# Keys of batches 1 to 3: loaded once by rows, transposed in pairs of heads, copied by VectorE into padded and 56-query tiles

## The chip, the cores and the metric

The kernel runs on one core of one Trainium2 chip. Its time is the device time of one execution in microseconds (us). Several executions of a kernel are taken and their median is given. One further number comes from an execution under the hardware profiler, with a record of every instruction: the span in it runs from the first to the last instruction, and the execution's own time is a little longer than its span.

The engines are named as the profile names them: PE is TensorE (matmul), PEld its weight load, DVE is VectorE, ACT is ScalarE, POOL is GpSimd, and SP is SyncE, which only issues transfers here. [...]

## The reference

The computation is an attention followed by a mixture of four experts. Of eight heads, three ("retrieval": 0, 2, 6) see all earlier keys, and five ("streaming": 1, 3, 4, 5, 7) see the first 4 keys (the sinks) and the last 64.

```python
# q, k, v: (4 batches, 8 heads, 768 rows, 64); n_sink = 4, window = 64
scores = scale * np.matmul(q, k.transpose(0, 1, 3, 2))
causal = rel >= 0                       # rel = query row - key row
stream_keep = causal & (is_sink | (rel < window))
mask = np.where(is_retrieval, causal, stream_keep)
a = softmax(np.where(mask, scores, -1e9))
x = np.matmul(a, v)                     # heads side by side: (3072, 512)

p = domain_probs / (domain_probs.sum(-1, keepdims=True) + 1e-09)
for e in range(4):                      # 3072 tokens, 512 -> 1024 -> 512
    h = np.maximum(x @ w1[e], 0.0)
    out += p[:, e:e + 1] * (h @ w2[e])
```

## The kernel before

**Stages.** The attention is cut into eight stages g = 2b + c: batch b (0 to 3) and half c of its 768 rows (CH = 384 queries). A stage makes xT[g], 384 tokens by 512, which the experts use. The experts take tokens in pieces: 384 and 128 tokens the plain way (plain_steps; first layer L950, second L971), then ten pairs of 128 (pair_steps; first layer L1063, then a product of half-size blocks in seven parts, L1096, whose sums VectorE makes at L919, L1037 and L1117). The inputs of a pair are scaled by the probabilities, once for each expert: scale_inputs, L1029, into a double buffer xs.

**Order.** The order of each engine's instructions is written by hand, and each engine keeps it. attention(b, c) and moe_steps() are generators that yield an estimate of the TensorE time of what they have just issued. A loop at the end of the kernel advances the experts and puts in attention steps behind a plan (the table `plan`, with att_ns(a) as the assumed length of a stage). require(a) drains the stages up to a before their output is read. Work that should stand a little later in the order (the scaling of a streaming head's output, L762) goes through later() and is issued by tick() once 1300 ns of the estimate have gone by.

**A stage of batches 1 to 3** (by_dma, g = 2 to 7) takes its heads in the order 0, 2, 6, 1, 3, 5, 7, 4. scores(h), L627, multiplies key tiles with the transposed queries qT; ScalarE takes the exponential (L645) and VectorE multiplies by a mask (L649). values(h) or values_r(h), L739 and L675, follow one or two heads behind.

**Keys and queries.** Both have to lie with the head's 64 numbers on the partitions. Before the change:

- loads(g + 1) is called at the start of stage g. On POOL it loads the keys of the three retrieval heads (load_k, L229, into kRr, 128 x 3 x 64 each), the queries of all heads (L207, into q16, three transfers of 128 x 8 x 64), the retrieval heads' values, and the keys of the five streaming heads (L233, into kSr). These go in windows: seven tiles of 128 rows, each 55 rows beyond the last (WQ = 55), so that each key row is loaded about twice. The half of a key tile's columns that belongs to the other head of a pair is zero.
- After the fourth head of stage g (in stage 1: at its end), transpose_rows(g + 1) puts on SP three transposing transfers for the queries (L268) and one for kRr (L255, nine blocks of 128 x 128, into kR).
- After the last head's scores of stage g, transpose_windows(g + 1) puts on SP put_sinks for kSr (L249, in first halves only, and L250: the 4 sink rows into each of the seven windows) and one transposing transfer of kSr (L255, 35 blocks, into kS).

So each key tile of a stage was transposed by the DMA into the place from which PE reads it. kRr and kSr have one buffer each.

**Values** of streaming heads are loaded in windows too, one head after another as values(h) frees its tile (L281), and their sinks are put in by sink_rows after the second head of the stage (the same put_sinks). 

Of the kernel before, what the change touches and what calls it, by code (L numbers as in the profile page):

```python
# [17 lines left out]
def kernel(  # L18
# [34 lines left out]
    P = 128  # L53
# [22 lines left out]
    NT = S // TK  # L76
    TC = CH // TK
    assert NS <= R0 and NW == 64 and NS + NW <= TK
    WQ = 55
    WK = WQ + NW - 1  # L80
    WT = 7
    WO = P - WK + NW
    assert WT * WQ - 1 == CH and NS + WK <= P

    pers = ctx.enter_context(tc.tile_pool(name="pers", bufs=1))
    att = ctx.enter_context(tc.tile_pool(name="att", bufs=1))
# [55 lines left out]
    p_sb = pers.tile([P, NTILE, E], FP32, name="p_sb")  # L142


    kRr = pers.tile([P, NR, 3, P], FP16, name="kRr")
    kSr = pers.tile([P, WT, NSH, P], FP16, name="kSr")
    sinks = pers.tile([P, 1, NSH * P], FP16, name="sinks")
    k_sinks = sinks[0:NS, :, :]
    v_sinks = sinks[P // 2 : P // 2 + NS, :, :]

# [71 lines left out]
            ),  # L222
        )

    def load_k(b, c, heads):

        for h in heads:
            if RETR[h]:
                gp.dma_start(  # L229
                    out=kRr[:, RH.index(h), :, own(h)], in_=rows_of(k, b, h, c)  # L230
                )
            else:
                gp.dma_start(  # L233
                    out=kSr[:, :, SH.index(h), own(h)],
                    in_=windows_of(k, b, h, c),
                )

    qTs = {}

# [11 lines left out]
            out=x[0:NS, :, :], in_=src.to_broadcast([NS, WT, NSH * P])  # L251
        )

    def transpose_keys(x, xr):
        nc.sync.dma_start(  # L255
            out=x.rearrange("p t s x -> p (t s) x"),
            in_=xr.rearrange("p t s x -> p (t s x)"),
            transpose=True,
        )

    def transpose_windows(b, c):
        put_sinks(kSr, k_sinks, c)
        transpose_keys(windows(kSf), kSr)

    def transpose_rows(b, c):
        alloc_qT(b, c)
        for j in range(3):
            nc.sync.dma_start(  # L268
                out=qTs[b, c][:, :, j * P : (j + 1) * P],
                in_=q16[b, c][:, j, :, :].rearrange("p h d -> p (h d)"),  # L270
                transpose=True,
            )
        transpose_keys(kR[b % 2][:, c, :, :, :], kRr)

    def load_v(b, c, heads):
        for h in heads:
# [158 lines left out]
    def mask_w():  # L435


        gp.memset(mW, 1.0)
        gp.affine_select(
            out=mW, in_=mW, compare_op=ALU.is_ge, fill=0.0,  # L440
            base=NW - WO, pattern=[[0, WT + 2], [-1, WQ]], channel_multiplier=1,
        )
        gp.affine_select(
            out=mW, in_=mW, compare_op=ALU.is_ge, fill=0.0,
            base=WO - 1, pattern=[[0, WT + 2], [1, WQ]], channel_multiplier=-1,
        )
# [7 lines left out]
        gp.affine_select(  # L454
            out=mW[0:NS, 1, :], in_=mW[0:NS, 1, :], compare_op=ALU.is_ge, fill=0.0,
            base=WQ - 1 - NW, pattern=[[1, WQ]], channel_multiplier=-1,
        )

    mask_c(bC, 0.0, -60000.0)
# [48 lines left out]
    def attention(b, c):  # L508
# [72 lines left out]
        def score_tiles(h):  # L581
            if RETR[h]:
                if c == 0:
                    return [
                        (512, [(2, 0, 256, 128), (0, 128, 0, 384)], [(mC, 0, 0, 256)]),
                        (256, [(1, 0, 128, 256)], [(mC, 0, 0, 128)]),
                    ]
                return [
                    (512, [(5, 0, 256, 128), (3, 128, 0, 384)], [(mC, 0, 0, 256)]),
                    (512, [(4, 0, 128, 256), (0, 256, 0, 256)], [(mC, 0, 0, 128)]),  # L590
                    (512, [(0, 0, 256, 128), (1, 128, 0, 384)], []),
                    (384, [(2, 0, 0, 384)], []),
                ]
            if b:
                starts = [max(WQ * t - 1, 0) for t in range(WT)] + [CH]
                parts = [
                    (t, q0, q0, q1 - q0)
                    for t, (q0, q1) in enumerate(zip(starts, starts[1:]))
                ]
                return [(CH, parts, [(mWf, 1 + 2 * WQ * c, 0, CH)])]  # L600
# [121 lines left out]
        def values(h):  # L722
            if RETR[h]:
                yield from values_r(h)
                return
            ct, u = PLACE[h]
            if first and u == 1:
                ps = pO.tile([P, 512], FP32, name="pO", bufs=2)
            else:
                ps = pV.tile([P, 512], FP32, name="pV", bufs=2)  # L730
            if first:
                warm_up(ps, {3: 4, 4: 4, 5: 6, 7: 10}.get(h, 0), 256)
            work = []
            for es, parts in es_of[h]:
                for t, o, q0, nq in parts:
                    work.append((es, t, o, q0, nq))
            ns = 0
            for n, (es, t, o, q0, nq) in enumerate(work):
                nc.tensor.matmul(  # L739
                    out=ps[:, q0 : q0 + nq],  # L740
                    lhsT=v_tile(b, c, h, t),
                    rhs=es[:, o : o + nq],
                    start=(n == 0),
                    stop=(n == len(work) - 1),
                    skip_group_check=True,
                )
# [13 lines left out]

            def scale(r=r, ps=ps):
                nc.vector.tensor_tensor(  # L762
                    out=xT[g][r, ct, :], in0=ps[r, 0:CH], in1=rc[r, :], op=ALU.mult
                )

            if not pair:
                nc.scalar.activation(out=rc[r, :], in_=rc[r, :], func=AF.Exp, scale=-1.0)  # L767
                later(scale)
            elif u == 0:
                scale_of[0] = scale  # L770
            else:
                nc.scalar.activation(out=rc, in_=rc, func=AF.Exp, scale=-1.0)
                later(scale_of[0])
                later(scale)

            yield ns + (600.0 if g == 1 else 0.0)

# [39 lines left out]
        else:  # L817
# [5 lines left out]
            def behind_values(h):  # L823
                if more and not RETR[h]:
                    load_v(*more, [h])
            if not by_dma:
                yield from transposes(0)
                yield from transposes(1)

            waiting = []  # L830
            for n, h in enumerate(order):
# [7 lines left out]
                    behind_values(done)  # L839
                waiting.append(h)  # L840
                if n == 1 and by_dma:
                    sink_rows(b, c)
                if n == 3 and more and g > 1:
                    transpose_rows(*more)
# [2 lines left out]
            if more:  # L847
                if g == 1:
                    load_probs(pair0)
                    transpose_rows(*more)  # L850
                transpose_windows(*more)
            for h in waiting:
                yield from values(h)
                behind_values(h)
# [37 lines left out]
    clock = [0.0]  # L892
    LAG = 1300.0

    def later(op):
        behind.append((clock[0] + LAG, op))

    def tick(ns):
        clock[0] += ns
# [287 lines left out]
        tick(ns)  # L1187
    tick(LAG)

    zero(gp, kRr)  # L1190
    zero(gp, kSr)

    def loads(a):
        b, c = divmod(a, NCH)
        load_k(b, c, RH)
        load_q(b, c)
        if b == 1:
            one_values_r(gp, b, c)
        load_v(b, c, RH)
        load_k(b, c, SH)  # L1200

    UNIT = FTP * DMP * mm_ns(CH) + 3 * FTP * mm_ns(DM)
    ONE = E * (FTP * DMP * mm_ns(P) + FTP * mm_ns(DM))
    PAIR = E * FTP * DMP * mm_ns(PC) + 7 * KT * mm_ns(HN)

    def att_ns(a):
        ns = 3500.0 if a % NCH == 0 else 5600.0
        return ns + (1100.0 + HP * 3 * 400.0 + NSH * 600.0 if a < NCH else 0.0)

    first_pair = E * UNIT + ONE  # L1210
# [27 lines left out]
    def require(a):  # L1238
        drained = False
        while state["a"] <= a:  # L1240
            attention_step()
            drained = True
        if drained:
            tick(LAG)

    spent = 0.0
    for ns, share in moe_steps():
# [45 lines left out]
```

## Time and profile before

| | |
|---|---|
| Median of 13 runs | 398.26 us (395.15 to 401.73) |
| The profiled execution's own time | 399.77 us |
| Its span | 398.1 us, 9356 instructions |
| Mean granted clock of PE | 0.991 |
| DMA queue q0 (POOL's) | 102656 packets, 20.98 MB, 71.6% of 16 engines |
| DMA queue q1 (SP's) | 62756 packets, 24.65 MB, 32.7% of 16 engines |

The table's last two rows are the time that a queue's packets took, as a share of the time of 16 DMA engines over the span. Queues that are busy at once add up, so that the sum in a stretch can be over 1.

The transfers that the change touches, of the list of issues: 30 loads kSr<-in_k_dram of 112 KB, 18 loads kRr<-in_k_dram of 48 KB and 18 loads q<-in_q_dram of 128 KB on POOL; 18 transposes qT<-q, 6 transposes kR<-kRr and 6 transposes kS<-kSr on SP, with 3 sinks<-kSr and 6 copies of the sinks into kSr. How long one instruction keeps its issuing engine, by tile: kSr 0.98 us, kRr 0.78 us and q 0.90 us on POOL (medians); on SP qT 1.23 us, kR 2.85 us and kS 6.41 us.

A page of the profile is read in this way. Busy time tells which engine could be the bound; for an engine near its span, what it waited for is what can be won. Time that another engine waits costs nothing by itself. A wait is put down to what released it last.

### The profile page before, as it was taken

How to read it: one execution, taken by the hardware profiler on the slowest of the kernel's cores; microseconds unless marked ns; L12 is line 12 of the kernel's file. 1: busy time of each engine (PE TensorE's matmuls, PEld its weight loads, DVE VectorE, ACT ScalarE, POOL GpSimd, SP SyncE). 2: the span in 40 equal slices, each digit the busy share in tenths (PEclk: the TensorE clock that was granted, in tenths of full speed). 3: DMA queues.
4: the chain of work that ended last, by engine and by line, in shares of the span. 5: the costliest groups of instructions: out<-in, count | busy, mean ns of one | idle time of the engine just before them, and what ended most of it. 6: DMA issues, size and time to landing. Idle time of an engine off the chain costs nothing.

```text
span 398.1 us, 9356 instructions
## 1 busy us (share of the span) xinstructions
PE 378.1 (95%) x3814; PEld 313.5 (79%) x3814; DVE 219.4 (55%) x472; ACT 233.8 (59%) x476; POOL 138.9 (35%) x182
## 2 busy tenths in 40 slices
PE   7899999899399998999999999999999999999996
PEld 4754556467288887899988898889988898888885
DVE  7736787546166555665563566565654546454340
ACT  4754469446158677674675578574774568361641
POOL 8823764935227542760374004740300000000000
PEclk9999999999799999999999999999999999999999
DMA  9999999999999999999799767999890210110101
GB/s 164 162 208 199 192 190 150 172 152 132 167 122 121 151 152 111 151 171 159 97 159 131 120 97 50 162 173 140 98 179 2 69 54 12 53 54 2 54 0 54
DMA packets 167632, 47.67 MB, mean 120 GB/s; under 512 B 156493, under 2 KB 161317, under 8 KB 167589
## 3 DMA queue, kind: packets, MB, share of 16 engines
q0 software_dynamic: 102656, 20.98, 71.6%
q1 hardware_dynamic: 62756, 24.65, 32.7%
q10 hardware_dynamic: 2176, 1.44, 1.5%
q8 instruction: 30, 0.49, 0.5%
q14 instruction: 14, 0.11, 0.1%
HBM read 48.82 MB, written 6.34 MB: 139 GB/s over the span
## 4 chain that ended last, share of the span: by engine, by line
PE 64%; DMA 20%; issue 5%; POOL 4%; ACT 3%; DVE 2%; SPq 1%; POOLq 0%; ACTq 0%
PE pA L1063 28%; PE pO L1096 24%; DMA kS<-kSr 7%; DMA w2sb<-in_moe_w_dram 7%; PE pA L627 4%; DMA kR<-kRr 3%; PE pO L971 3%; PE pA L950 2%; PE pV L675 1%; PE pV L739 1%; ACT es L645 1%; DMA vS<-in_v_dram 1%; POOL kSr L233 1%; DMA vS<-sinks 1%; ACT rc L757 1%
## 5 line engine op out<-in xcount | busy, mean ns | idle before, releaser
L1063 PE MATMUL pA<-xs,w1sb 128*128 128x256 f16 x1280 | 148.6, 275 | 0.0
L1063 PEld LDWEIGHTS <-w1sb 128*128 128x128 f16 x1280 | 124.3, 99 | 15.3
L1072 ACT ACTIVATE hA<-pA 128x512 f16<-128x512 f32 x160 | 94.9, 597 | 42.0 <-PE pA L1063 39.6
L1096 PEld LDWEIGHTS <-hA 128*128 128x128 f16 x1120 | 105.7, 98 | 12.4
L645 ACT ACTIVATE es<-pA 128x384 f16<-128x384 f32 (+2 forms) x122 | 59.9, 511 | 41.2 <-PE pA L627 37.2
L1096 PE MATMUL pO<-w2sb,hA 128*128 128x256 f16 x640 | 79.0, 272 | 0.0
L1029 DVE TENSOR_TENSOR xs<-xT,pB 128x1024 f16<-128x1024 f16 (+1 forms) x52 | 49.6, 974 | 23.9 <-PE pA L1063 23.6
L1096 PE MATMUL pO<-tsb,hA 128*128 128x256 f16 x480 | 59.8, 272 | 0.0
L281 POOL DMA_DIRECT2D vS<-in_v_dram x30 | 29.3, 982 | 80.7 <-PE pV L739 46.4
L919 DVE TENSOR_TENSOR hA<-hA 128x1024 f16<-128x1024 f16 (+1 forms) x80 | 41.4, 553 | 1.0
L233 POOL DMA_DIRECT2D kSr<-in_k_dram x30 | 29.5, 988 | 25.5 <-DMA kS<-kSr 13.9
L963 ACT ACTIVATE hA<-pA 128x384 f16<-128x384 f32 (+1 forms) x64 | 22.1, 386 | 20.7 <-PE pA L950 14.4
L950 PE MATMUL pA<-xT,w1sb 128*128 128x384 f16 (+1 forms) x256 | 31.7, 273 | 1.9 <-ACT hA L963 1.8
L971 PE MATMUL pO<-w2sb,hA 128*128 128x512 f16 x128 | 30.6, 379 | 0.6 <-DMA w2sb<-in_moe_w_dram 0.6
L649 DVE TENSOR_TENSOR es<-es,mS 128x384 f16<-128x384 f16 (+1 forms) x40 | 13.7, 348 | 31.2 <-ACT es L645 31.1
L649 DVE TENSOR_TENSOR es<-es,mC 128x256 f16<-128x256 f16 (+1 forms) x42 | 10.6, 257 | 33.8 <-ACT es L645 33.4
L950 PEld LDWEIGHTS <-w1sb 128*128 128x128 f16 x256 | 19.3, 98 | 10.1 <-issue 2.4
L1114 ACT COPY s<-pO 128x256 f32<-128x256 f32 x30 | 11.2, 373 | 25.1 <-PE pO L1096 23.5
L762 DVE TENSOR_TENSOR xT<-pV,rc 64x384 f16<-64x384 f32 x37 | 20.4, 554 | 9.0 <-ACT rc L767 6.8
L627 PE MATMUL pA<-qT,kR 128*128 128x384 f16 (+2 forms) x120 | 24.0, 278 | 1.2 <-ACT qT L538 0.4
L1037 DVE TENSOR_TENSOR hA<-hA 128x512 f16<-128x512 f16 (+1 forms) x30 | 15.3, 510 | 16.9 <-ACT hA L1072 16.7
L627 PE MATMUL pA<-qT,kS 128*128 128x55 f16 (+4 forms) x255 | 16.8, 196 | 7.5 <-DMA kS<-kSr 6.9
(113 smaller groups left out, 336.5 us busy)
## 6 DMA issues: line engine op xcount, KB each, us to landing
pB<-p_rows SPq DMA_DIRECT2D x10, 512.0 KB, 4.6
out_dram<-o SPq DMA_DIRECT2D x19, 256.0 KB, 2.7
w1sb<-in_moe_w_dram POOLq DMA_DIRECT2D x8, 512.0 KB, 9.6
w2sb<-in_moe_w_dram POOLq DMA_DIRECT2D x4, 1024.0 KB, 13.1
kSr<-in_k_dram POOLq DMA_DIRECT2D x30, 112.0 KB, 6.9
vS<-in_v_dram POOLq DMA_DIRECT2D x30, 112.0 KB, 4.2
q<-in_q_dram POOLq DMA_DIRECT2D x18, 128.0 KB, 9.1
vR<-in_v_dram POOLq DMA_DIRECT2D x24, 48.0 KB, 6.7
```

The source lines that it names most:

```text
L233: gp.dma_start(out=kSr[:, :, SH.index(h), own(h)], in_=windows_of(k, b, h, c),)
L281: gp.dma_start(out=t[:, :, own_v(h)], in_=windows_of(v, b, h, c))
L627: nc.tensor.matmul(out=ps[:, o : o + nq], lhsT=key_tile(b, c, h, t), rhs=qTs[b, c][:, hp, q0 : q0 + nq], start=(n == 0 or not first), stop ...
L645: nc.scalar.activation(out=es[:, 0:cols], in_=ps[:, 0:cols], func=AF.Exp, scale=SC)
L649: nc.vector.tensor_tensor(out=es[:, o0:o1], in0=es[:, o0:o1], in1=m[:, mo : mo + o1 - o0], op=ALU.mult,)
L919: nc.vector.tensor_tensor(out=out, in0=a, in1=b, op=ALU.subtract)
L950: nc.tensor.matmul(out=pss[ft][:, 0:cols_n], lhsT=w1sb[:, e * DMP + ct, ft * P : (ft + 1) * P], rhs=x[:, ct, :], start=(n == 0), stop=(n = ...
L971: nc.tensor.matmul(out=ps_o, lhsT=hs[:, ft, j * P : (j + 1) * P], rhs=w2sb[:, e * FTP + ft, :], start=(ft == 0), stop=(ft == FTP - 1),)
L1029: nc.vector.tensor_tensor(out=o, in0=xin, in1=pb.to_broadcast([P, DMP, n, P]), op=ALU.mult)
L1063: nc.tensor.matmul(out=ps[:, f * PC : (f + 1) * PC], lhsT=w1sb[:, e * DMP + ct, (f0 + f) * P : (f0 + f + 1) * P], rhs=xs[:, ct, :], start= ...
L1072: nc.scalar.activation(out=blocks[:, b0 : b0 + 2, k0 : k0 + 2, :].rearrange("p t f x -> p f t x"), in_=ps.rearrange("p (f t x) -> p f t x" ...
L1096: nc.tensor.matmul(out=ps, lhsT=a[:, k, :], rhs=b(k), start=(first and k == 0), stop=(k == KT - 1), skip_group_check=not first,)
```

## The change

From batch 1 on:

- **Loads.** kRr, kSr and the key sinks' buffer go. The keys of all eight heads are loaded once, by rows, as the queries are: three transfers of 128 x 8 x 64 into k_rows. All the keys stand first in loads(), ahead of the queries.
- **Transposes.** transpose_rows(g + 1) puts six transposing transfers on SP, three for k_rows into a new tile kT (four pairs of heads by 128 + 384 columns, the last 384 written) and three for the queries. transpose_windows goes, and with it what stood at the end of a stage.
- **Copies on VectorE.** At the start of stage g, keys_to_rows copies the retrieval heads' halves of kT into kR (two copies: 64 x 768 and 64 x 384). After the second head, before sink_rows, keys_to_windows copies the streaming heads' halves into the seven overlapping windows in kS (three copies: 2 x 7 x 124, the same again, and 7 x 124 elements on 64 partitions), in first halves also the 4 sinks (three small copies), and moves the last 80 columns of kT to its front for the next half (128 x 4 x 80; not in the last stage).
- **Tiles of 56.** WQ becomes 56, so that the windows start at even elements; the masks and the first tile's length follow (WF).
- **Order.** att_ns is 500 larger, with a yield of 500 behind keys_to_rows. later() takes the stage with it, and require(a) now issues all that is still waiting of stages up to a.
- **Zeros.** Instead of kRr and kSr, kR's second buffer and the first 80 columns of kT are zeroed, on POOL.

```diff
-    WQ = 55
+    WQ = 56
     WK = WQ + NW - 1
     WT = 7
-    WO = P - WK + NW
+    WF = WT * WQ - CH
+    WO = P - WQ + WF
...
-    kRr = pers.tile([P, NR, 3, P], FP16, name="kRr")
-    kSr = pers.tile([P, WT, NSH, P], FP16, name="kSr")
+    kT = pers.tile([P, HP, P + CH], FP16, name="kT")
...
+    def load_k(b, c):
+        k_rows[b, c] = att.tile([P, 3, H, D], FP16, name="k_rows", bufs=1)
+        load_by_rows(k, k_rows[b, c], b, c)
...
-    def transpose_windows(b, c):
-        put_sinks(kSr, k_sinks, c)
-        transpose_keys(windows(kSf), kSr)
...
     def transpose_rows(b, c):
         alloc_qT(b, c)
-        for j in range(3):
-            nc.sync.dma_start(
-                out=qTs[b, c][:, :, j * P : (j + 1) * P],
-                in_=q16[b, c][:, j, :, :].rearrange("p h d -> p (h d)"),
-                transpose=True,
-            )
-        transpose_keys(kR[b % 2][:, c, :, :, :], kRr)
+        for x, xr, at in ((kT, k_rows[b, c], P), (qTs[b, c], q16[b, c], 0)):
+            for j in range(3):
+                nc.sync.dma_start(
+                    out=x[:, :, at + j * P : at + (j + 1) * P],
+                    in_=xr[:, j, :, :].rearrange("p h d -> p (h d)"),
+                    transpose=True,
+                )
...
+    def keys_to_rows(b, c):
+
+        for n, hps in ((slice(0, 2), slice(0, 2)), (slice(2, 3), slice(3, 4))):
+            nc.vector.tensor_copy(
+                out=kR[b % 2][half(0), c, n, :, :].rearrange("p n t x -> p n (t x)"),
+                in_=kT[half(0), hps, P : P + CH],
+            )
+
+    def keys_to_windows(b, c):
+
+        x = windows(kSf)
+        for r, n0, hp0, n in ((1, 0, 0, 2), (1, 3, 2, 2), (0, 2, 2, 1)):
+            r = half(r)
+            src = kT[r, hp0 : hp0 + n, P - WO + NS :]
+            step = src.ap[1][0]
+            src = bass.AP(
+                src.tensor, src.offset, [src.ap[0], [step, n], [WQ, WT], [1, P - NS]]
+            )
+            dst = x[r, :, n0 : n0 + n, :].rearrange("p t n x -> p n t x")
+            nc.vector.tensor_copy(out=dst[:, :, :, NS:P], in_=src)
+            if c == 0:
+                src = kT[r, hp0 : hp0 + n, P : P + NS]
+                src = src.rearrange("p n (t x) -> p n t x", t=1)
+                nc.vector.tensor_copy(
+                    out=dst[:, :, :, 0:NS], in_=src.to_broadcast([D, n, WT, NS])
+                )
+        if b * NCH + c + 1 < G:
+            nc.vector.tensor_copy(out=kT[:, :, P - WO : P], in_=kT[:, :, CH + P - WO :])
...
-            if not by_dma:
+            if by_dma:
+                keys_to_rows(b, c)
+                yield 500.0
+            else:
                 yield from transposes(0)
                 yield from transposes(1)
...
                 if n == 1 and by_dma:
+                    keys_to_windows(b, c)
                     sink_rows(b, c)
...
                 if g == 1:
                     load_probs(pair0)
                     transpose_rows(*more)
-                transpose_windows(*more)
...
-    zero(gp, kRr)
-    zero(gp, kSr)
+    zero(gp, kR[1].rearrange("p c n t x -> p (c n) t x"))
+    gp.memset(kT[:, :, P - WO : P], 0.0)
...
-        load_k(b, c, RH)
+        load_k(b, c)
         load_q(b, c)
         if b == 1:
             one_values_r(gp, b, c)
         load_v(b, c, RH)
-        load_k(b, c, SH)
...
-        ns = 3500.0 if a % NCH == 0 else 5600.0
+        ns = 4000.0 if a % NCH == 0 else 6100.0
...
         if drained:
             tick(LAG)
+        while any(g <= a for _, _, g in behind):
+            behind.pop(0)[1]()
```

More of the change, by code (lines that the diff above doesn't have):

```diff
@@ L78 @@
     assert NS <= R0 and NW == 64 and NS + NW <= TK
-    WQ = 55
+    WQ = 56
     WK = WQ + NW - 1
     WT = 7
-    WO = P - WK + NW
-    assert WT * WQ - 1 == CH and NS + WK <= P
+    WF = WT * WQ - CH
+    WO = P - WQ + WF
+    assert NS + WK <= P and WO % 2 == 0
     pers = ctx.enter_context(tc.tile_pool(name="pers", bufs=1))
@@ L142 @@
     p_sb = pers.tile([P, NTILE, E], FP32, name="p_sb")
-    kRr = pers.tile([P, NR, 3, P], FP16, name="kRr")
-    kSr = pers.tile([P, WT, NSH, P], FP16, name="kSr")
-    sinks = pers.tile([P, 1, NSH * P], FP16, name="sinks")
-    k_sinks = sinks[0:NS, :, :]
-    v_sinks = sinks[P // 2 : P // 2 + NS, :, :]
+    kT = pers.tile([P, HP, P + CH], FP16, name="kT")
+    v_sinks = pers.tile([NS, 1, NSH * P], FP16, name="v_sinks")
     x_pair = pers.tile([P, 3, P], FP16, name="x_pair")
@@ L223, in load_triples @@
         )
[L225 to L230, printed above, removed]
-                )
[L232 to L236, printed above, removed]
+    k_rows = {}
+    def load_k(b, c):
+        k_rows[b, c] = att.tile([P, 3, H, D], FP16, name="k_rows", bufs=1)
+        load_by_rows(k, k_rows[b, c], b, c)
     qTs = {}
@@ L252, in put_sinks @@
         )
[L254 to L257, printed above, removed]
-            transpose=True,
-        )
-    def transpose_windows(b, c):
-        put_sinks(kSr, k_sinks, c)
-        transpose_keys(windows(kSf), kSr)
     def transpose_rows(b, c):
         alloc_qT(b, c)
-        for j in range(3):
-            nc.sync.dma_start(
-                out=qTs[b, c][:, :, j * P : (j + 1) * P],
-                in_=q16[b, c][:, j, :, :].rearrange("p h d -> p (h d)"),
-                transpose=True,
-            )
-        transpose_keys(kR[b % 2][:, c, :, :, :], kRr)
+        for x, xr, at in ((kT, k_rows[b, c], P), (qTs[b, c], q16[b, c], 0)):
[5 more added lines that the diff above has]
+                )
+    assert RH == [0, 2, 6] and SH == [1, 3, 4, 5, 7]
+    def keys_to_rows(b, c):
[3 more added lines that the diff above has]
+                in_=kT[half(0), hps, P : P + CH],
+            )
+    def keys_to_windows(b, c):
[17 more added lines that the diff above has]
+            nc.vector.tensor_copy(out=kT[:, :, P - WO : P], in_=kT[:, :, CH + P - WO :])
     def load_v(b, c, heads):
@@ L440, in mask_w @@
             out=mW, in_=mW, compare_op=ALU.is_ge, fill=0.0,
[L441 removed]
+            base=NW - 1 + WF - WO, pattern=[[0, WT + 2], [-1, WQ]], channel_multiplier=1,
         )
@@ L444, in mask_w @@
             out=mW, in_=mW, compare_op=ALU.is_ge, fill=0.0,
-            base=WO - 1, pattern=[[0, WT + 2], [1, WQ]], channel_multiplier=-1,
+            base=WO - WF, pattern=[[0, WT + 2], [1, WQ]], channel_multiplier=-1,
         )
@@ L455, in mask_w @@
             out=mW[0:NS, 1, :], in_=mW[0:NS, 1, :], compare_op=ALU.is_ge, fill=0.0,
-            base=WQ - 1 - NW, pattern=[[1, WQ]], channel_multiplier=-1,
+            base=WQ - WF - NW, pattern=[[1, WQ]], channel_multiplier=-1,
         )
@@ L594, in score_tiles @@
             if b:
-                starts = [max(WQ * t - 1, 0) for t in range(WT)] + [CH]
+                starts = [max(WQ * t - WF, 0) for t in range(WT)] + [CH]
                 parts = [
@@ L599, in score_tiles @@
                 ]
-                return [(CH, parts, [(mWf, 1 + 2 * WQ * c, 0, CH)])]
+                return [(CH, parts, [(mWf, WF + 2 * WQ * c, 0, CH)])]
             if c == 0:
@@ L767, in values @@
                 nc.scalar.activation(out=rc[r, :], in_=rc[r, :], func=AF.Exp, scale=-1.0)
-                later(scale)
+                later(scale, g)
             elif u == 0:
@@ L772, in values @@
                 nc.scalar.activation(out=rc, in_=rc, func=AF.Exp, scale=-1.0)
-                later(scale_of[0])
-                later(scale)
+                later(scale_of[0], g)
+                later(scale, g)
             yield ns + (600.0 if g == 1 else 0.0)
@@ L893, with later @@
     LAG = 1300.0
-    def later(op):
-        behind.append((clock[0] + LAG, op))
+    def later(op, g):
+        behind.append((clock[0] + LAG, op, g))
     def tick(ns):
```

## The prediction

> **What bounds the kernel.** I read first the busy shares and the row of forty slices, then the list of who waited for whom on PE, then the chain that ended last, and last SP's and VectorE's own timelines around the one hole that the slices show.
>
> ```profile
> PE 378.1 (95%) x3814; PEld 313.5 (79%) x3814; DVE 219.4 (55%) x472; ACT 233.8 (59%) x476; POOL 138.9 (35%) x182
> ...
> PE   7899999899399998999999999999999999999996
> ...
> PEclk9999999999799999999999999999999999999999
> ```
>
> PE works for 378.1 of 398.1 us, so the end moves only by what PE loses, 20.0 us in all. Slices are 9.95 us long. Apart from the start and the end there is one hole, slice 11 (99.5 to 109.5 us), and there alone the granted clock falls. VectorE (55%) and POOL (35%) have room on average. PE's waits name the hole:
>
> ```profile
> PE pA L627 <- DMA kS<-kSr: 6.9, 1, 6.9
> PE pV L739 <- DVE xT L762: 2.2, 5, 0.7
> ...
> PE pA L627 <- DMA kR<-kRr: 0.4, 1, 0.4
> ```
>
> One wait of 6.9 us, once: the first scores of a streaming head of batch 1 stand at the transposed key windows. All that VectorE makes PE wait in the later stages is the second row, in five pieces. The chain continues from the wait:
>
> ```profile
> 92.09 14.41 DMA kS<-kSr
> 106.55 0.51 PE pA L627 x7
> 107.06 3.41 PE pA L1063 x16
> 110.47 0.33 PE pV L675 x6
> 110.80 2.79 PE pA L1063 x24
> ```
>
> Sixteen L1063 matmuls take 3.41 us here and 1.75 us elsewhere in this chain; seven L627 take 0.51 instead of 0.36; the 24 take 2.79 instead of 2.62. The windows of time say why (columns: PE, PEld, DVE, ACT, POOL busy with counts, then granted clock, DMA share, GB/s):
>
> ```profile
> 104.00:106.00 2.00, 0.00 (x0) 0.00 (x0) 0.00 (x0) 0.00 (x0) 0.00 (x0) 0.55 1.67 97
> 106.00:108.00 2.00, 1.45 (x13) 1.14 (x14) 0.31 (x1) 0.49 (x1) 0.97 (x1) 0.50 0.93 179
> 108.00:110.00 2.00, 2.00 (x11) 1.44 (x10) 1.25 (x3) 0.60 (x1) 2.00 (x4) 0.50 0.84 152
> 110.00:112.00 2.00, 2.00 (x20) 1.67 (x18) 1.72 (x6) 0.71 (x2) 1.96 (x3) 0.74 1.88 122
> ```
>
> The idle PE is granted half its clock. The excess is 1.66 + 0.15 + 0.17 us, and 0.2 for the six L675 (0.54 us in the timeline, 0.34 later): 2.15 us. So the hole costs 6.91 + 2.15 = **9.06 us**. SP's timeline tells what made the windows late:
>
> ```profile
> 69.95 4.55 SPq L268 DMA_TRANSPOSE qT<-q  x3
> 74.67 2.88 SPq L255 DMA_TRANSPOSE kR<-kRr  x1
> 82.94 0.63 SPq L249 DMA_DIRECT2D sinks<-kSr  x1
> 83.61 0.71 SPq L250 DMA_DIRECT2D kSr<-kSr  x1
> 92.09 7.70 SPq L255 DMA_TRANSPOSE kS<-kSr  x1
> ```
>
> Five kSr loads (POOL, 68.1 to 73.0) must land before the sinks can be copied (82.94), then the sinks' copy must land (92.09), and only then the 35-block transpose starts, 14.41 us to the end. These are four transfers in series on queues that carry more than one transfer's share (DMA share 1.3 to 2.1 from 70 to 110 us).
>
> **The change, part by part.**
>
> *Loads on POOL (six stages, batch 1 to 3).* Gone: 30 kSr at 988 ns and 18 kRr at 775 ns, 29.5 + 14.0 = 43.5 us. New: 18 k_rows in the shape of the q loads, 896 ns each, 16.1 us. POOL loses 27 us, and with them its 13.9 + 11.6 us of waits for the old transpose before kSr. POOL bounds nothing: on the path this is 0. Runs of 64 elements go from 30 x 896 + 18 x 384 = 33,792 to 18 x 1,024 = 18,432, 15% of the queue's 102,656 packets. But for stage 2 the order matters: k_rows has 1,920 runs more than kRr *ahead of* q, while kSr's 4,480 behind q are gone. kSr's 4,480 runs took 70.8 to 82.9 us, 2.7 ns each, so q lands 5.2 us later, its last part at about 76 instead of 70.8 (issued 59.2, landed 11.6 later); everything behind q lands about 7 us earlier.
>
> *Transposes on SP.* Gone per stage: kR (9 blocks, 1.3 to 4.1 us of SP), kS (35 blocks, 5.9 to 7.7) and the key sinks' one or two copies (0.65 each). New: three kT, each four blocks like a qT (1.23 us). A stage falls from 56 blocks to 24, and SP gains some 6 us. Behind these on SP stand x_one and x_pair's transposes, pB's load and the stores; they can only come earlier, and PE waited for none of them.
>
> *First scores of stage 2.* In the built order they stand behind 36 more layer matmuls than before, about 2.6 us, so kR and qT are wanted at 87.3 + 2.6 = 89.9 us instead of 87.3. The transposes: kT from about 70 (when the rows have landed), done on SP at 75; qT from 76 to 80. How long they take to land has two rows: 12.9 us (kR, from 74.67, amid kSr and vS loads) and 3.8 us (qT at 102.8). By the first qT ends at 93, a wait of 3 us; by the second at 84, none. The load of vS is still there, kSr's not; I take 0.5 us, and lose the old 0.37 us.
>
> *VectorE copies.* No copy of fp16 from SBUF to SBUF is in the trace; the nearest are three one-input fp16 instructions, by shape:
>
> ```profile
> L858 DVE TENSOR_SCALAR mS<-early 128x480 f16<-128x480 f16 x1 | 0.3, 277 | 0.0
> ...
> L858 DVE TENSOR_SCALAR mC<-early 128x256 f16<-128x256 f16 x1 | 0.2, 227 | 0.0
> L858 DVE TENSOR_SCALAR mS<-early 128x160 f16<-128x160 f16 x1 | 0.2, 195 | 0.0
> ```
>
> (277 - 195) / 320 = 0.26 ns an element, and 154 ns fixed. The other end is a converting copy out of PSUM, L561, 64x384 in 540 ns: about 1.0 ns an element. At the first slope: the padded rows 768 and 384 elements, 351 + 252 = 0.60 us; the windows 2x7x124 twice and 7x124 once, 599 x 2 + 376 = 1.57; sinks in first chunks 3 x 0.17; the carry of 320, 0.24. A stage has a burst of 2.3 us (first chunk) or 1.8 (second), and 0.6 ahead of it: 15.8 us in all, VectorE 219 to 235 us. At the second slope a burst is about 6 us, 43 us in all. I take the first: same type, same memory, dense rows of 124.
>
> On the path? The windows are ready long before use: the burst follows head 2's last mask, and the first window scores follow 64 layer matmuls later, 64 x 0.109 = 7 us. They also stand 3.5 us later than before. What the burst hides behind is slack of whatever is queued after it, and that is head 6's mask and the next scale_inputs (L1029, 1.22 us). xs for expert e+1 may be written only once e-1 is read, and is read 32 matmuls (3.5 us) later, so its slack is 3.5 - 1.2 = 2.3 us less what is ahead of it: in the timeline 1.3 (at 175 us) to 1.8 us (at 97.5). A burst of 2.3 us at the worst moment overruns by up to 1 us, and mostly not at all. Six stages: 0 to 6 us, I take **1.5**. keys_to_rows waits for kT in VectorE's order; behind it stand L987 or L1117, which free pO. In stages 3 to 7 kT was issued half a stage earlier, 15 us or more, so it doesn't wait.
>
> [...]
>
> *Masks, 56-query tiles, the ordering of later, yield of 500, att_ns, memsets.* The same seven matmuls per head and 384 columns; POOL's memsets shrink by about 1 us; the recorded order shifts by under 4 us and ends at the same place. 0.
>
> **Sum** against the profiled execution's own 399.77 us (span 398.1 and 1.67 around it): - 9.06 - 0.37 + 0.5 + 1.5 = 392.3. That execution lies 1.5 us above the median of 398.26. Whether its hole was longer than usual or something else isn't shown, so I take off half: **391.6 us**.
>
> **Rivals.**
> 1. *The wait moves, not goes:* qT lands late and stage 2's first scores wait 3 to 5 us instead, at an idle long enough for the clock to fall. For: the 12.9 us row, and q behind larger loads. Against: kSr's loads gone, 2.6 us of grace. 391.6 + 4 = 395.5, up to 397.5 (no change).
> 2. *VectorE becomes the bound in the bursts (slower).* At the L561 slope a burst is 6 us against 1.3 to 2.3 of slack: 3 to 4 us lost in each of six stages, 20 us, with 9 gained: about 407. The point from which it decides is 1.5 us lost a stage, a burst of 3.6 us, about 0.5 ns an element. For: 64 partitions, short pieces of 124. Against: the L858 rows, and VectorE's 45% idle time. Half-way, 400 to 403.
> 3. *The hole was that run's own:* the thirteen runs spread by 6.6 us, so others may lose only 3 us there; then the gain against the median is 3 to 4 us, 394.5.
>
> **Chances.** Forecast 58% (own range 388.5 to 394), rival 1 14%, rival 3 10%, rival 2 18%. About 0.5% (2 us) is what can be told from no change here. Faster by more: 0.58, with 0.09 and 0.08 from rivals 1 and 3: 0.75. Same 0.09, the rest of these with a little of rival 2. Slower 0.16. The range, 387.5 to 400, takes rivals 1 and 3 whole and leaves out most of rival 2.
>
> **What would show it.** Right: no PE wait on kS or kT over 1 us, the granted clock at 1.00 in every slice, the kS<-kT copies at about 0.6 us for 2x7x124, PE's idle time some 11 us instead of 20, VectorE near 235 us. [...]

## The result, and the profile after

| | median | lowest to highest | ratio to before (95%) |
|---|---|---|---|
| before | 398.05 us | 395.11 to 401.73 (48 runs) | |
| changed | 394.05 us | 391.21 to 398.60 (11 runs) | 0.9876 (0.9841 to 0.9910) |

The changed kernel is 1.2% faster. A ratio compares undisturbed runs alone (of the changed kernel eight, with four of 397.45 to 398.60 us left out as slow) and the medians take all, so a ratio is not quite the quotient of two medians. Where a ratio is turned into microseconds below, it is taken of 398.05: here -4.9 us (-6.3 to -3.6).

The profiled execution took 394.51 us, with a span of 392.8, against 399.77 and 398.1 before: 5.3 us less. Its page, first the busy shares and the forty slices of 9.82 us, then the two large queues:

```profile
PE 376.4 (96%) x3814; PEld 312.8 (80%) x3814; DVE 231.9 (59%) x516; ACT 234.5 (60%) x476; POOL 110.2 (28%) x152
...
PE   7889899879999997999999999999999999999996
...
PEclk9999999989999999999999999999999999999999
...
q0 software_dynamic: 86816, 19.01, 57.2%
q1 hardware_dynamic: 38156, 18.13, 20.7%
```

Slice 11, the hole of the kernel before, is full, and the clock there is whole. But there is a new dent in slice 9 (78.6 to 88.4 us), and there the granted clock falls. (The 7 in slice 16 stands where L774's waits are, at the end of a stage; before it was an 8, with shorter waits.) PE stands idle for 16.4 us instead of 20.0. Both queues carry less, and POOL has lost 28.7 us of work, without being what sets the end. PE's waits (engine, line and tile, released by; then us in total, times, longest):

```profile
PE pA L965 <- ACT hA L978: 3.6, 1, 3.6
PE pV L751 <- DVE xT L774: 3.4, 6, 0.8
```

No row names kS, kR, kT or qT from batch 1 on. The long wait is a single one, for ScalarE, in the plain experts, some 25 us ahead of where the old hole stood. The chain that ended last between 58 and 90 us says what held ScalarE (start, duration, what):

```profile
58.73 14.20 DMA k_rows<-in_k_dram
72.93 0.02 issue
72.94 7.06 DMA kT<-k_rows
80.00 0.02 issue
80.02 0.02 ACTq L1008
...
80.46 0.29 ACT hA L978
...
80.79 1.86 PE pA L965 x16
```

A transpose of keys that VectorE first copies at 91.0 us lands at 80.00 us, and what it releases is line 1008 on ScalarE's queue: a *store* of finished output. Behind that store in ScalarE's order stands L978, which makes hA for PE. The windows of time show the idle PE and then its clock (columns as in the prediction):

```profile
78.00:80.00 2.00, 0.00 (x0) 0.00 (x0) 1.12 (x2) 0.00 (x0) 1.11 (x2) 1.00 2.46 171
80.00:82.00 2.00, 1.21 (x12) 1.21 (x12) 0.00 (x0) 1.22 (x6) 1.79 (x4) 0.64 1.98 206
82.00:84.00 2.00, 2.00 (x11) 1.06 (x9) 0.00 (x0) 0.68 (x3) 1.59 (x6) 0.51 1.75 161
84.00:86.00 2.00, 2.00 (x25) 1.47 (x24) 0.88 (x2) 0.65 (x3) 2.00 (x3) 1.00 1.24 294
```

A wait of 3.58 us is followed by about half the clock from 80 to 84 us. The sixteen L965 take 1.86 us instead of 1.06 (as at 76.15 us), and the eight L986 behind them 2.47 instead of 1.73 to the next start: the hold costs 3.58 + 0.80 + 0.74 = 5.1 us.

**Why a store waits for a transpose.** In the kernel before, the first three stores of the plain experts (L993 there) stood at the same place. ScalarE's timeline and PE's at that place, of the kernel *before*:

```profile
73.04 4.90 ACTq L993 DMA_DIRECT2D out_dram<-hA  x3
77.99 1.70 ACT L963 ACTIVATE hA<-pA 128x128 f16<-128x128 f32 x8 [5.47 <-DVE tsb L919]
...
78.32 1.05 PE L950 MATMUL pA<-xT,w1sb 128*128 128x128 f16 x16 [1.75 <-ACT hA L963]
```

There ScalarE stood 4.90 us at the three stores, PE waited 1.75 us, and the clock stayed at 1.00. The difference is in what the stores wait for. The records of the two traces name the semaphore by which each transfer of SP and ScalarE tells of its landing: the same eight in both, numbers 100, 102 and 104 to 109, each carried by 15 of the 120 transfers before, by 14 or 15 of the 117 in the changed kernel. Along SP's list, with ScalarE's eight transfers put in between, they come in turn. Ahead of each of the three stores ScalarE waits for the semaphore that the store itself carries, and this wait ended when the earlier transfer with that number had landed (us):

| | store | semaphore | earlier transfer with it | landed | wait ended |
|---|---|---|---|---|---|
| before, L993 | first | 100 | x_pair's transpose | 72.18 | 72.20 |
| | second | 102 | pB's load | 74.61 | 74.63 |
| | third | 104 | first qT | 77.53 | 77.55 |
| changed, L1008 | first | 102 | pB's load | 74.72 | 74.74 |
| | second | 105 | second kT | 79.19 | 79.21 |
| | third | 106 | third kT | 80.00 | 80.02 |

In both kernels six transfers on SP lie between pB's load and the stores in that turn; but in the changed one the two copies of the value sinks stand among the stores and take 100 and 104, so that the stores draw 102, 105 and 106.

In the changed kernel VectorE's sums for the second and third store had been ready at 75.4 and 77.1. In the kernel before, the sum for the third had been ready at 76.5. (The row above puts ScalarE's idle time down to L919, which only happened to end shortly before.) So the kernel before had the same kind of hold, only about 1.1 us long instead of 2.9. Its trace showed that much before the change; the prediction did not look there.

### The profile page after: what moved, and what is told of

Read it like the earlier page. It is cut to its first block, busy times and chain, and to the rows that moved or that the text cites. A ratio compares the mean times of both kernels' runs of the same rounds, so it can differ in the third digit from the quotient of the medians.

```text
span 392.8 us, 9368 instructions
## 1 busy us (share of the span) xinstructions
PE 376.4 (96%) x3814; PEld 312.8 (80%) x3814; DVE 231.9 (59%) x516; ACT 234.5 (60%) x476; POOL 110.2 (28%) x152
## 4 chain that ended last, share of the span: by engine, by line
PE 74%; DMA 16%; POOL 4%; ACT 3%; issue 1%; DVE 1%; ACTq 0%; POOLq 0%
PE pA L1078 36%; PE pO L1111 29%; DMA w2sb<-in_moe_w_dram 7%; DMA vS<-in_v_dram 4%; PE pA L639 4%; DMA k_rows<-in_k_dram 4%; PE pO L986 2%; PE pA L965 2%; DMA kT<-k_rows 2%; PE pV L687 1%; PE pV L751 1%; POOL vS L297 1%; ACT rc L769 1%; ACT es L657 1%; DVE xT L774 1%
## 5 line engine op out<-in xcount | busy, mean ns | idle before, releaser
L1078 PE MATMUL pA<-xs,w1sb 128*128 128x256 f16 x1280 | 146.4, 273 | 0.0
L1111 PE MATMUL pO<-w2sb,hA 128*128 128x256 f16 x640 | 78.1, 272 | 0.0
L1044 DVE TENSOR_TENSOR xs<-xT,pB 128x1024 f16<-128x1024 f16 (+1 forms) x52 | 49.6, 972 | 23.6 <-PE pA L1078 23.6
L978 ACT ACTIVATE hA<-pA 128x384 f16<-128x384 f32 (+1 forms) x64 | 22.3, 386 | 25.9 <-PE pA L965 16.8
L965 PE MATMUL pA<-xT,w1sb 128*128 128x384 f16 (+1 forms) x256 | 32.2, 278 | 3.7 <-ACT hA L978 3.6
L986 PE MATMUL pO<-w2sb,hA 128*128 128x512 f16 x128 | 31.3, 386 | 1.1 <-DMA w2sb<-in_moe_w_dram 1.1
L965 PEld LDWEIGHTS <-w1sb 128*128 128x128 f16 x256 | 19.9, 101 | 12.1 <-issue 4.2
L774 DVE TENSOR_TENSOR xT<-pV,rc 64x384 f16<-64x384 f32 x37 | 20.4, 553 | 10.2 <-ACT rc L779 8.0
L1132 DVE TENSOR_TENSOR o<-pO,s 128x256 f32<-128x256 f32 x30 | 12.6, 422 | 20.9 <-PE pO L1111 12.6
L769 ACT ACTIVATE rc<-pV,eps 64x384 f32<-64x384 f32 x37 | 21.3, 576 | 4.9 <-PE pV L751 4.2
```

The lines of the kernel that those rows point to most:

```text
L769: nc.scalar.activation(out=rc[r, :], in_=ps[o, 0:CH], func=AF.Ln, bias=eps[o, :])
L774: nc.vector.tensor_tensor(out=xT[g][r, ct, :], in0=ps[r, 0:CH], in1=rc[r, :], op=ALU.mult)
L965: nc.tensor.matmul(out=pss[ft][:, 0:cols_n], lhsT=w1sb[:, e * DMP + ct, ft * P : (ft + 1) * P], rhs=x[:, ct, :], start=(n == 0), stop=(n = ...
L986: nc.tensor.matmul(out=ps_o, lhsT=hs[:, ft, j * P : (j + 1) * P], rhs=w2sb[:, e * FTP + ft, :], start=(ft == 0), stop=(ft == FTP - 1),)
L1044: nc.vector.tensor_tensor(out=o, in0=xin, in1=pb.to_broadcast([P, DMP, n, P]), op=ALU.mult)
L1078: nc.tensor.matmul(out=ps[:, f * PC : (f + 1) * PC], lhsT=w1sb[:, e * DMP + ct, (f0 + f) * P : (f0 + f + 1) * P], rhs=xs[:, ct, :], start= ...
```

## The experiments

**The hold, away.** The store of the plain experts goes to SP, in the changed kernel (e1) and in the kernel before (e2):

```diff
-                nc.scalar.dma_start(out=out[nt * P : (nt + 1) * P, :], in_=acc[nt])
+                nc.sync.dma_start(out=out[nt * P : (nt + 1) * P, :], in_=acc[nt])
```

> The changed kernel with one edit: the four stores of the plain experts' results are issued on SP's queue, not on ACT's. Theory (ACT's in-order queue stands at a store whose transfer slot is still held by a kT transpose, and PE then waits for ACT's L978): the wait PE <- ACT of 3.6 us at 77 to 81 us goes, and with it 1.7 us of half clock; about 389.5 us, 4 to 5 less than the changed kernel. Rival (the wait comes from the loaded transfer queues or from PE's own work, the stores are only beside it): no difference, 393 to 395 us.

Measured: 389.28 us (388.84 to 389.75), ratio 0.9771 (0.9726 to 0.9817), -9.1 us. ScalarE's and SP's timelines of this kernel:

```profile
76.91 1.84 ACT L978 ACTIVATE hA<-pA 128x128 f16<-128x128 f32 x8 [4.04 <-PE pA L965]
...
79.77 12.31 SPq L1008 DMA_DIRECT2D out_dram<-hA  x4
```

ScalarE waits for PE now, and not PE for ScalarE; no single wait of PE is above 1.8 us. SP itself stands 12.3 us at the stores, and nobody needs it then. So the hold was worth 4.2 us (0.9876 - 0.9771, of 398.05) or 4.8 by the medians, against the 5.1 of the profile.

> The kernel before with the same edit. It has a wait of 1.75 us for ACT at the same place. Theory (the hole before kS ends at the time at which a transfer lands, which PE's speed ahead of it does not move): the 1.75 us go, the hole at kS grows by as much, 397.5 to 398.5 us. Rival (the waits add up): 396 us.

Measured: 398.34 us (395.90 to 401.97), 0.9994 (0.9959 to 1.0029). The time is unchanged, but its hole is another one. PE's waits, and the timelines of SP and ScalarE:

```profile
PE pA L1063 <- ACT hA L1072: 7.3, 1, 7.3
...
91.90 7.89 SPq L255 DMA_TRANSPOSE kS<-kSr  x1
99.89 1.99 SPq L993 DMA_DIRECT2D out_dram<-hA  x4
...
103.23 1.57 ACT L1072 ACTIVATE hA<-pA 128x512 f16<-128x512 f32 x3 [8.94 <-DMA out_dram<-hA]
```

On SP the stores stand behind the waiting kS transpose. What is stored lies in hA's buffer, so the pairs' layers may not write there until the stores have read it. The serial key transfers hurt again, through a third tile. This is therefore not a clean control.

**The change cut in two.** e3 is the kernel before with the order's edits alone; its PE order is that of the changed kernel:

```diff
-            if not by_dma:
+            if by_dma:
+                yield 500.0
+            else:
...
-        ns = 3500.0 if a % NCH == 0 else 5600.0
+        ns = 4000.0 if a % NCH == 0 else 6100.0
...
+        while any(g <= a for _, _, g in behind):
+            behind.pop(0)[1]()
```

e4 is the changed kernel with att_ns as before and without the yield; its PE order is that of the kernel before.

> The kernel before with nothing but the changed kernel's recorded order (att_ns 500 larger, a yield of 500 at a stage's start, the stage given to later and drained by require); PE's order is then the changed kernel's, instruction for instruction. First window scores of stage 2 stand 32 layer matmuls (3.5 us) later. Theory (most of the gain comes from the transfers that go): the hole at kS is 3.4 us instead of 6.9 and may be too short for the clock to fall: 393.5 to 395.5 us, and a wait on kS is still there. Rival (the gain is the order's alone): 394 us and less, no wait on kS left. Third (order does nothing): 398 us.

Measured: 393.44 us (392.53 to 397.94), 0.9901 (0.9862 to 0.9941), -3.9 us. PE's waits:

```profile
PE pA L952 <- ACT hA L965: 2.0, 1, 2.0
PE pA L627 <- DMA kS<-kSr: 1.6, 1, 1.6
```

The old hole has shrunk from 6.9 to 1.6 us with all the old transfers in place. PE comes to the windows at 103.06 us instead of 99.64, and they land at 104.64 instead of 106.55. So 3.42 us of the 5.33 are the order's shift. The other 1.91 come from a transpose that started later (93.53 us instead of 92.09) but let PE go 11.11 us after its start instead of 14.46; whether the order did that is not shown. After the shorter wait the clock holds: the window from 104 to 106 us has 1.00, where the kernel before had 0.55.

> The changed kernel with the order of the kernel before (att_ns as before, no yield behind keys_to_rows); PE's order is the earlier kernel's. Theory (the transfers carry the gain, kT and qT have landed before stage 2's first scores even 2.6 us earlier): no wait on kS, at most 1 us on kR or qT, 393.5 to 395 us. Rival (the order carries the gain): a new wait of 2 us or more at stage 2's first scores or at the windows, 396 to 398 us.

Measured: 400.64 us (398.63 to 402.68), 1.0070 (1.0041 to 1.0100): *slower* than before by 2.8 us (1.6 to 4.0). PE's waits and two pieces of the chain:

```profile
PE pA L964 <- ACT hA L977: 4.6, 1, 4.6
PE pA L639 <- DVE kR L261: 3.2, 6, 1.1
...
PE pA L964 <- DMA w1sb<-in_moe_w_dram: 2.2, 1, 2.2
...
74.06 8.67 DMA kT<-k_rows
...
83.52 1.86 PE pA L964 x16
```

The wait at kS is gone here too. In its place come the hold on ScalarE, 4.6 us with half the clock behind it, and six waits, one at the start of each of six stages, for the copies into kR, 3.2 us, which the changed kernel's order hides. (The wait for w1sb, 2.2 us, lies at another place; other kernels' traces have none there or up to 1.0 us.) My theory that the transfers carry the gain fell: as the kernel is written, the order carries it, and the transfers by themselves lose. The rival came nearer in time, but not in place: what waits at the first scores waits for VectorE's copies, and none at the windows is left.

**Both halves, with the hold away.**

> The transfers alone (earlier order) with the stores on SP's queue. Theory (of the 2.6 us that the transfers alone lost, the stores' hold on ACT is the cause: a wait of 4.6 us and about 4 us of half clock, against 1.75 us before): 391.5 to 393 us, 8 to 9 less than the transfers alone; left are some 3 us of waits for keys_to_rows' copies, which have no yield ahead of the scores. Rival (VectorE's copies and the key loads ahead of w1 cost most): 396 us or more.

Measured (e4 with the stores on SP): 393.50 us (393.39 to 394.52), 0.9888 (0.9839 to 0.9936). The hold's wait is gone and kR's remains (3.6 us in six). This is half a microsecond above what I expected, and 7.1 us below e4.

> The earlier transfers in the new order, with the stores on SP's queue. Theory (on SP the stores stand behind the 35-block transpose of kSr, which holds that queue to about 102 us, and the experts' ScalarE writes wait for the stores to read hA): no gain over the order alone, 393 to 396 us, with a PE wait on ACT near 100 us. Rival (the stores' place helps whatever the transfers): 391 us.

Measured (e3 with the stores on SP): 400.53 us (399.35 to 403.28), 1.0044 (1.0008 to 1.0079), worse than I had expected from any theory. The chain of this kernel:

```profile
95.18 4.00 SPq L255
...
99.28 3.81 DMA out_dram<-hA
...
103.19 0.61 ACT hA L1074
...
103.84 5.28 PE pA L1065 x24
```

It is e2's chain again: kS's transpose holds SP, the stores stand behind it, hA is held, and PE waits 8.7 us and then runs 24 matmuls in 5.28 us that take 2.62 earlier in the same chain. To move a store to SP was right only where SP had no long waiter ahead of it (the changed kernel gained 4.2 us by it in e1, the order alone lost 5.7 in e6). So I freed ScalarE in another way: the first three stores stay on ScalarE but are issued later, when the next piece's third expert begins, in e3 (e9), the changed kernel (e10) and the kernel before (e11):

```diff
+        while held and nt0 == 3 and e == 2:
+            n = held.pop(0)
+            nc.scalar.dma_start(out=out[n * P : (n + 1) * P, :], in_=acc[n])
...
-                nc.scalar.dma_start(out=out[nt * P : (nt + 1) * P, :], in_=acc[nt])
+                if nt < 3:
+                    held.append(nt)
+                else:
+                    nc.scalar.dma_start(out=out[nt * P : (nt + 1) * P, :], in_=acc[nt])
```

> The order alone (earlier transfers), with the first three stores of the plain experts left on ACT's queue and issued 7 us later in its order (ahead of expert 2 of the fourth tile), so that neither ACT's L963 work nor SP's queue stands at them. Theory (what remains is the wait for kS, which ends when a transfer lands; PE comes 2 us earlier and waits 2 us longer): 392.5 to 394 us, no gain over the order alone. Rival (the stores' hold and the wait for kS add up): 391 us.

> The changed kernel with the same late stores on ACT. Theory (the hold on ACT was all that kept the changed kernel from its gain): 389 to 390 us, as with the stores on SP. Rival (it was SP's queue that made the difference): 394 us.

> The kernel before with the same late stores on ACT. Theory (the hole at kS is bounded by when the transfer lands): 397.5 to 399 us, no gain. Rival (waits add up): 396 us.

Measured: e9 393.93 us, 0.9864 (0.9816 to 0.9912); e10 389.70 us, 0.9767 (0.9724 to 0.9810); e11 398.26 us, 0.9948 (0.9905 to 0.9990). PE waits for ScalarE there no more in e10, 0.5 us in e9. In e11 the hold has moved with the stores: ScalarE stands 4.34 us at them from 81.40 us on, and PE waits 2.25 us there instead of 1.75 at the old place. The hole at kS is a little shorter. PE's waits, then ScalarE's and PE's timelines in e11:

```profile
PE pA L627 <- DMA kS<-kSr: 5.5, 1, 5.5
PE pA L954 <- ACT hA L967: 2.2, 1, 2.2
...
81.40 4.34 ACTq L946 DMA_DIRECT2D out_dram<-hA  x3
...
86.17 1.05 PE L954 MATMUL pA<-xT,w1sb 128*128 128x128 f16 x16 [2.25 <-ACT hA L967]
```

Two different ways of taking the stores out of ScalarE's way (e1, e10) give the same time, which is what ties the loss to that place and not to SP's load. All eight cells, by their ratios:

| | stores as written | stores moved |
|---|---|---|
| kernel before | 0 | -2.1 us (e11; PE still waits for the stores) |
| order alone | -3.9 us (e3) | -5.4 us (e9) |
| transfers alone | +2.8 us (e4) | -4.5 us (e5) |
| both: the change | -4.9 us | -9.3 us (e10), -9.1 us (e1) |

Each cell is uncertain by 1.2 to 1.9 us; e1 and e5 have the stores on SP, e9 to e11 late on ScalarE. With the hold away (the right column without e11), the order is worth 4.6 us on top of the transfers (e5 to e1), and the transfers 3.9 on top of the order (e9 to e10); each is 4.2 by the medians. Read down the left column, the order alone gives 3.9 and the transfers on top of it 1.0, which can't be told from nothing; on top of the transfers the order gives 7.7. Read across, the stores in ScalarE's way cost 7.3 us where the transfers came without the new order and 4.2 to 4.4 in the changed kernel. Without the new transfers no such cost is shown: e9 against e3 is 1.5 us by the ratios and nothing by the medians, and e11 did not take the hold away.

**VectorE's bursts, twice and none.** e7 and e8 are e1 with the copies into the windows made twice, and left out. In e8 the windows and sinks are not refreshed after batch 0, so that the streaming heads of batches 1 to 3 multiply batch 0's keys; the rest of the work is there.

```diff
-        for r, n0, hp0, n in ((1, 0, 0, 2), (1, 3, 2, 2), (0, 2, 2, 1)):
+        for r, n0, hp0, n in 2 * ((1, 0, 0, 2), (1, 3, 2, 2), (0, 2, 2, 1)):
```

> The changed kernel with the stores on SP, and the window and sink copies of each stage done twice: bursts of 4.2 us in first halves and 3.4 in second ones instead of 2.3 and 1.8. Theory of the prediction (slack behind a burst is 1.3 to 2.3 us, and a single burst overruns by a quarter of a us a stage): 391 to 394 us, with PE waits on xs behind the bursts. Rival (VectorE has room for either): no change, 389 to 390 us.

> The changed kernel with the stores on SP, without the copies into the windows and their sinks (kS keeps batch 0's keys, so that streaming heads of later batches get wrong scores); 12 us of VectorE's work goes. Theory of the prediction (the bursts cost 1.5 us, most of it in those copies): 388 us. Rival (they are free): 389.3 us, no change.

Measured: twice 393.64 us (391.23 to 394.55), 0.9876 (0.9818 to 0.9934); none 388.85 us (388.13 to 391.80), 0.9779 (0.9720 to 0.9839). Against e1's 389.28, one burst costs 0.4 us by the medians and nothing by the ratios: it can't be told from zero. With a second burst the median of four runs is 4.4 us higher. Its profile has a new wait, 2.1 us for xs (L1044) in three pieces, the longest of them 1.6 us at 102.32, right behind a burst. So the slack holds one burst, and the second overruns it. Most of the rest of the 4.6 us by which this profiled execution's span is longer than e1's lies ahead of all bursts: the five matmuls on kR that e1 starts at 60.45 us start at 62.41 here. A longer wait for w2sb (2.0 us instead of 1.2) is part of it, and the mean granted clock is 0.996 instead of 0.999, with 1.00 in every window from 60 to 120 us. So 2 us is what the trace shows for the second burst.

## Why the prediction was right, and where it failed

Forecast 391.6 us, range 387.5 to 400; measured 394.05. Side and range hold; the gain was 4.0 to 4.9 us instead of 6.7. The time lies just above the forecast's own part of the range (388.5 to 394), where rivals 3 and 1 stood (394.5 and 395.5). That it came so near is in part luck: in the profiled execution, forecast at 392.3 and measured at 394.5, the hold and L774's waits took 4.6 us that stood at 0, and the 2.0 us set down for the first scores and the bursts did not show.

- **The hole at the key windows goes: right.** No wait for kS is left, slice 11 is full, its clock whole. The serial transfers were its cause in the sense that with them gone it goes, also in the earlier order (e4). Taking them out was not the only cure: see the order below. The sign "the granted clock at 1.00 in every slice" failed, in slice 9.
- **The failed step** is the one on SP: "Behind these on SP stand x_one and x_pair's transposes, pB's load and the stores; they can only come earlier, and PE waited for none of them." It followed SP's own queue and stopped there. The three stores ahead of L978 are on ScalarE's queue, and share completion semaphores with SP's transfers (105 and 106 with the second and third kT). The third of them came later: ScalarE's L978 began at 80.46 us instead of 77.99, PE waited 3.58 us instead of 1.75, and the clock fell to 0.64 and 0.51 in the two windows from 80 to 84 us. The kernel before already showed the hold: 1.1 us of ScalarE's stand there was for a qT transpose, and as much of PE's 1.75 us (L950 <- ACT) followed from it. The cost over before is 1.83 + 0.80 + 0.74 = 3.4 us. e1 and e10 show it: without the hold, 389.3 to 389.7. Rival 1 had the kind of loss right, a moved wait long enough for the clock, and the size (+4), but at the wrong place: stage 2's first scores waited for neither kT nor qT.
- **The order at 0: wrong**, though it shifts by "under 4 us", as I wrote. e3 gains 3.9 us by it alone: 3.42 us of shift and an earlier landing leave a wait of 1.58 us, and the clock holds. On top of a sum that had already taken out the whole hole, the shift would have counted the same gain twice, which is why the forecast survived. But with the new transfers the order is worth 4.6 us even with the hold away, most of it the waits at kR's copies, 3.2 us in e4 and 3.6 in e5: it is not bookkeeping.
- **First scores of stage 2, +0.5:** no wait of the kind is in the trace. **Bursts, +1.5:** 0.4 by the medians of e8 and e1, which can't be told from nothing; neither trace's list of PE's waits has one for xs.
- **The copies' rate: right.** By form (after the bar: busy us, mean ns, idle before):

```profile
L277 DVE COPY kS<-kT 64x1736 f16<-64x1736 f16 x12 | 7.1, 608 | 0.2
L261 DVE COPY kR<-kT 64x768 f16<-64x768 f16 x6 | 2.7, 455 | 0.1
L277 DVE COPY kS<-kT 64x868 f16<-64x868 f16 x6 | 2.5, 410 | 0.1
L261 DVE COPY kR<-kT 64x384 f16<-64x384 f16 x6 | 2.0, 325 | 0.0
```

The windows were priced at 599 and 376 ns from L858's slope and took 608 and 410, so rival 2, VectorE as the bound, never started. All seven kinds of copy sum to 17.1 us against 15.8. VectorE ended at 231.9 us, 3 below the forecast. The copies into kR were priced at 351 and 252 ns and took 455 and 325 in the mean; at two stage starts they took 345 and 244, and three longer ones (806, 756 and 480 ns) make the difference. The last section has what is known of it.

- **In the sum of the profiled execution:** -9.06 - 0.37 + 3.4 (the hold) + 1.2 (L774's waits, 2.2 to 3.4 us) = -4.8, against -5.3 measured. The 0.5 us between is not accounted for. L774's longer waits were not forecast, and no run singles them out; e3 has 2.6, e4 and e5 2.7, e9 3.3, e1 3.4.
- **PE's idle time, 11 us forecast, was 16.4.** The hold is 1.8 of that, but e1 still has 13.4 (387.8 - 374.4). The forecast had also taken off the 2.15 us of half clock, which is busy time and no idle time: from its own terms 20.0 - 6.9 - 0.4 = 12.7 was due.
- **Rival 3, the hole was that run's own:** the hole is not in one execution alone, since e11, with the same PE order and key transfers, has it too (5.5 us). How much it varies from run to run is not shown; there is one trace of each kernel. The *new* hole may well vary. Of the eight compared runs of the changed kernel, two had a mean granted clock of 1.000 and took 391.21 and 391.96 us; six with 0.991 to 0.996 took 392.94 to 395.06. But the clock falls elsewhere too (0.994 in e10's profiled execution, which has no hold), so that the faster two waited less at the stores is not shown.

The fastest kernels here are e1 and e10, the changed kernel with the stores off ScalarE's path at that place: 2.3% below before, and about 1.1% below the change as written.

## What to carry to other kernels

When transfers are added to or removed from one queue, read what *every* DMA of the neighbouring queues waits for in the built order, not only what stands behind the change: a store that shares completion semaphores can hold its engine for a transfer that has nothing to do with it (here ScalarE, 2.9 us, for the third kT). Put stores on a queue where nothing urgent stands behind them, and look first at what stands ahead of them there (e1 against e2 and e6). And when a change mixes a mechanism with a shift in order, run each alone: here the order alone gave nearly all of the gain, and the mechanism alone lost, until one hold was taken away.

## What the hardware showed that I had not expected

**Copies beside POOL's loads.** The copies into the windows met no load of POOL's, and those into kR met ten, which were no longer than elsewhere (vS 0.98 to 0.99 us, k_rows 0.90, vR 0.78 to 0.81; all eighteen k_rows took 876 to 913 ns). What differs is the length of the copies. The pair of copies into kR in the changed kernel, at two stages' starts, and then what POOL did at the first of them:

```profile
121.61 1.03 DVE L261 COPY kR<-kT 64x768 f16<-64x768 f16 x2
...
289.80 0.51 DVE L261 COPY kR<-kT 64x768 f16<-64x768 f16 x2
```

```profile
121.61 0.98 POOL L293 DMA_DIRECT2D vS<-in_v_dram  x1 [0.51 <-issue]
```

Beside POOL's loads of vS the pair took 1.03 us (121.61) and 0.97 (154.58); with POOL at rest 0.51 (289.80). But at 201.47 us a pair took 0.51 too, with POOL's loads of vR (0.79 us) going on, so what makes a pair longer is not shown. In the sum it is small: both kinds together came to 4.7 us instead of 3.6.

**Where the clock lets go.** Idle stretches of 1.75 us (before, at the stores) and 1.58 us (e3, at kS) left the clock at 1.00; one of 3.58 us (changed, at the stores) was followed by 0.64 and 0.51 in the windows from 80 to 84 us. So 1.83 us more of waiting cost 3.4 us of time. But the length of a wait alone does not settle it: 2.25 us (e11, at the stores) left the clock at 1.00 from 84 to 92 us, while e10, whose longest wait is one of 2.0 us (for vS), has a mean of 0.994, with 1.00 in every window from 76 to 108 us. Where it fell there, and what else decides, is not shown here.
